# Two 1 MB tiles of the second layer asked for in five pieces of rows each

## The chip, the cores and the metric

The kernel runs on one core of a Trainium2 chip. The metric is the device time of one execution in microseconds (us), the median of several runs. The core has five engines that run their own instruction streams: PE (TensorE, matrix multiplication), DVE (VectorE), ACT (ScalarE), POOL (GpSimd) and SP (SyncE, which here does nothing but ask for transfers). Data come from the chip's main memory (HBM) into the on-chip memory by 16 DMA engines. A transfer is asked for by one instruction on SP and is finished when all its parts have landed; other engines learn of that from a semaphore.

## The reference

Two layers of a decoder that makes one token for each of 8 sequences: attention with 32 query heads over 4 groups of cached keys and values (4096 positions, 128 numbers each), and a dense layer with GELU. Both layers use the same weights and the same caches, all in 32-bit floats.

```python
def _A_ref(x, k_cache, v_cache, wq, wo):
    q = (x @ wq).reshape(B, Sq, Hq, Dh).transpose(0, 2, 1, 3)
    k = jnp.repeat(k_cache, rep, axis=1)
    v = jnp.repeat(v_cache, rep, axis=1)
    scores = jnp.einsum("bhqd,bhkd->bhqk", q, k) * (Dh ** -0.5)
    p = _softmax(scores, axis=-1)
    o = jnp.einsum("bhqk,bhkd->bhqd", p, v)
    return o.transpose(0, 2, 1, 3).reshape(B, Sq, Hq * Dh) @ wo

def _B_ref(x, w1, b1, w2, b2):
    h = _gelu(jnp.einsum("bsd,df->bsf", x, w1) + b1)
    return jnp.einsum("bsf,fd->bsd", h, w2) + b2

x = x + _A_ref(_layernorm(x), ...)   # layer 0
x = x + _B_ref(_layernorm(x), ...)
x = x + _A_ref(_layernorm(x), ...)   # layer 1
x = x + _B_ref(_layernorm(x), ...)
```

## The kernel before

Everything that is read passes through the arena, one tile of 128 partitions by 52 units; a unit is 1024 floats per partition (`SCW`, line 34), 512 KB over all partitions. A slot of the arena is 2, 4 or 8 units, so a transfer is 1, 2 or 4 MB; one of 2 units has rows of 8192 bytes, one row for each partition. The caches and weights lie in HBM in the order in which the tiles are read, so each row of a tile is one contiguous piece.

`stream` (line 255) is the list of all transfers in their order. It is filled before the first instruction (lines 770 to 796): wq, then for each sequence of layer 0 its K and V tiles, wo (`o0`), w1 (`i0`), w2, and then layer 1 with the sequences in reverse order, wo (`o1`), w1 (`i1`) and what is left of w2 (`late`). Each entry has a key, a size in units, its source and the units at which it may lie. `pump` (line 258) goes through the list in order: as long as the next entry's units are free, it takes the slot and issues one transfer on SP (line 268); the first entry without a place stops it. `release` (line 273) frees a slot after its last use and calls `pump` again. So the order of transfers is that of `stream`, and the moment of one is set by the buffer that it waits for.

All these transfers share SP's queue. The framework counts their completion on eight semaphores in turn (DMAHW0 to DMAHW7 in the order of instructions), so a transfer also waits until the one eight places before it, which used the same semaphore, has landed, where no other wait has shown that already.

The users of the two tiles that the change touches: `scores` (line 586) multiplies a K tile into the scores of one sequence, in layer 1 for sequence 6 with the tile ("k", 6, 3, 1) as the last of that sequence's eight pieces of K; it is 2 units at unit 36 (the list for `batch(1, last_b - 1, ...)`, line 786). `project` (line 418) multiplies the attention's output by wo; in layer 1 `o1` comes in six tiles of 8, 8, 8, 4, 2 and 2 units (line 791), numbered 0 to 5. After it comes `expand("i1")` (line 287), which multiplies by w1 (`i1`, tiles of five times 4, three times 2, and 1, 0.5 and 0.5 units, line 792; line 303 for the wide part, 306 for the rest) and, between these, by w2 (`down_row`, line 468, matmuls at line 472). Both end in one addition (line 846) and the transfer of the result (line 848).

Of the kernel before, what the change touches and what calls it, by code (L numbers as in the profile page):

```python
# [14 lines left out]
P = 128  # L15
# [34 lines left out]
Q_AT = (0, (B + 1) * QW - 32, (B + 1) * QW - 8, 32)  # L50
KEEP = SCW + CH + 3 * P
DMA_SCRATCH = 64


class Arena:
# [50 lines left out]
def decode_layers(ctx: ExitStack, tc: tile.TileContext, x, kc, vc, wq, wo, w1, w2, out):  # L106


    nc = tc.nc
# [148 lines left out]
    def pump():  # L258
        while stream:
            key, k, src, starts, keys = stream[0]  # L260
            if not k:
                slot = Kept(starts)
            else:
                slot = arena.take(k, [i for i in starts if i + k <= arena.limit])
            if slot is None:
                return
            stream.pop(0)
            nc.sync.dma_start(out=slot.ap[:, 0:src.shape[1]], in_=src)
            slot.cols = src.shape[1]
            slot.keys = keys  # L270
            held[key] = slot

    def release(slot):
        if slot.keys:
            held.update(slot.parts())
            return
        slot.free()
        pump()
# [424 lines left out]
    def opened():  # L703
        arena.limit = N_UNIT
        pump()
# [87 lines left out]
    for e, n in LATE:  # L793
        w = LATE_C * Q4
        at, to = CB * NFT * Q4 + e * w, LATE_AT * SCW + e * w
        stream.append((("late", e), 0 if e else LATE_C, w2[0][:, at:at + n * w], arena.ap[:, to:to + n * w] if e else (LATE_AT,), ()))
    pump()
    rs = layernorm(x_row, rsum)
    queries(rs)
# [123 lines left out]
```

## Time and profile before

| what | value |
|---|---|
| median of 3 runs | 848.6 us (847.54 to 849.02) |
| the profiled execution's own time | 848.87 us |
| its span, first to last instruction | 847.0 us |
| granted TensorE clock, mean | 0.821 of full speed |
| read from HBM in the span | 357.78 MB, 423 GB/s on average |
| transfers on SP's queue | 136 |
| TensorE, busy time on `scores` (L595) and `values` (L638) | 162.3 us and 87.4 + 84.9 us |

The span is shorter than the execution's own time, because what lies before the first and after the last instruction isn't in it. In the page's slices a digit is the busy share of one 21 us slice in tenths, and the DMA row is the mean over the 16 DMA engines. A queue's row has its packets, its megabytes and the time that its packets took as a share of 16 engines' span. In rows of instructions, what stands in brackets is the idle time of the engine just ahead and what ended it.

### The profile page before, as it was taken

How to read it: one execution, taken by the hardware profiler on the slowest of the kernel's cores; microseconds unless marked ns; L12 is line 12 of the kernel's file. 1: busy time of each engine (PE TensorE's matmuls, PEld its weight loads, DVE VectorE, ACT ScalarE, POOL GpSimd, SP SyncE). 2: the span in 40 equal slices, each digit the busy share in tenths (PEclk: the TensorE clock that was granted, in tenths of full speed). 3: DMA queues.
4: the chain of work that ended last, by engine and by line, in shares of the span. 5: the costliest groups of instructions: out<-in, count | busy, mean ns of one | idle time of the engine just before them, and what ended most of it. 6: DMA issues, size and time to landing. Idle time of an engine off the chain costs nothing.

```text
span 847.0 us, 9470 instructions
## 1 busy us (share of the span) xinstructions
PE 535.8 (63%) x4120; PEld 179.1 (21%) x4120; DVE 192.4 (23%) x636; ACT 55.4 (7%) x118; POOL 2.4 (0%) x14
## 2 busy tenths in 40 slices
PE   0755565656656657677778775476666576655677
PEld 0221111111111111133243222111111121212334
DVE  0013132313222231300010242232414132222011
ACT  0110000000000000000201100000000000000021
POOL 0000000000000000000000000000000000000000
PEclk9977779676876877699999897968768768788899
DMA  9999999999999999999999999999999999999997
GB/s 402 420 423 430 433 433 431 426 436 427 424 428 435 434 432 421 427 429 424 429 409 413 399 427 438 429 430 435 425 438 426 434 429 433 431 426 434 421 426 285
DMA packets 19768, 358.51 MB, mean 423 GB/s; under 512 B 2192, under 2 KB 2576, under 8 KB 4112
## 3 DMA queue, kind: packets, MB, share of 16 engines
q1 hardware_dynamic: 19584, 357.77, 99.2%
q8 instruction: 32, 0.52, 0.3%
q10 hardware_dynamic: 144, 0.15, 0.1%
q14 instruction: 8, 0.07, 0.0%
HBM read 357.78 MB, written 0.13 MB: 423 GB/s over the span
## 4 chain that ended last, share of the span: by engine, by line
DMA 73%; PE 23%; DVE 2%; issue 1%; another core or an unknown queue 1%; ACT 0%; SPq 0%; ACTq 0%; DVEq 0%
DMA arena<-in_k_dram 28%; DMA arena<-in_v_dram 21%; DMA arena<-in_w_dram 10%; DMA arena<-in_wo_dram 8%; PE sps L595 8%; PE o_ps L638 7%; DMA arena<-in_wq_dram 5%; PE y L424 2%; PE acc L361 1%; PE sps L472 1%; PE acc L306 1%; PE sps L650 1%; PE acc L303 0%; PE sps L346 0%
## 5 line engine op out<-in xcount | busy, mean ns | idle before, releaser
L595 PE MATMUL sps<-arena,qz 128*32 128x512 f32 x1024 | 162.3, 777 | 118.9 <-DMA arena<-in_k_dram 117.0
L638 PE MATMUL o_ps<-arena 128*32 128x512 f32 x512 | 87.4, 816 | 48.2 <-DMA arena<-in_v_dram 36.7
L638 PE MATMUL o_ps<-arena,spare 128*32 128x512 f32 x512 | 84.9, 782 | 40.9 <-DMA arena<-in_v_dram 34.0
L595 PEld LDWEIGHTS sps<-arena,qz 128*32 128x32 f32 x1024 | 37.7, 132 | 208.2 <-issue 169.8
L643 DVE SCALAR_TENSOR_TENSOR scr<-o_ps,bits,scr 128x128 f32<-128x128 f32 x192 | 67.3, 351 | 6.8
L641 DVE TENSOR_SCALAR scr<-o_ps,bits 128x128 f32<-128x128 f32 x64 | 22.4, 351 | 144.6 <-PE o_ps L638 144.6
L424 PE MATMUL y<-arena,oxT 128*32 128x256 f32 x512 | 37.8, 441 | 23.5 <-DMA arena<-in_wo_dram 23.5
L361 PE MATMUL acc<-arena,oxT 128*32 128x512 f32 x248 | 32.9, 671 | 6.3 <-DMA arena<-in_wq_dram 4.9
L650 PEld LDWEIGHTS sps<-bits,scr 128*128 128x128 f32 x128 | 21.7, 213 | 67.6 <-issue 48.3
L638 PEld LDWEIGHTS o_ps<-arena 128*32 128x32 f32 x512 | 16.9, 134 | 81.4 <-issue 49.1
L638 PEld LDWEIGHTS o_ps<-arena,spare 128*32 128x32 f32 x512 | 17.2, 131 | 71.7 <-issue 47.1
L600 DVE TENSOR_SCALAR_CACHE_REDUCE arena<-sps 128x512 f32<-128x512 f32 x16 | 11.1, 691 | 91.4 <-PE sps L595 91.4
L651 DVE TENSOR_TENSOR oxT<-sps,scr 128x8 f32<-128x8 f32 x64 | 10.5, 164 | 87.1 <-PE sps L650 87.1
L600 DVE TENSOR_SCALAR_CACHE_REDUCE spare<-sps 128x512 f32<-128x512 f32 x16 | 11.1, 691 | 82.4 <-PE sps L595 82.4
L619 ACT ACTIVATE sps<-arena,bits 128x512 f32<-128x512 f32 x16 | 10.9, 681 | 285.2 <-DVE scr L613 285.2
L619 ACT ACTIVATE sps<-spare,bits 128x512 f32<-128x512 f32 x16 | 10.9, 681 | 263.6 <-DVE scr L613 263.6
L650 PE MATMUL sps<-bits,scr 128*128 128x8 f32 x128 | 27.6, 288 | 0.0
L424 PEld LDWEIGHTS y<-arena,oxT 128*32 128x32 f32 x512 | 18.0, 125 | 44.0 <-DMA arena<-in_wo_dram 25.9
L303 PE MATMUL acc<-arena,oxT 128*32 128x512 f32 x160 | 20.7, 631 | 9.2 <-DMA arena<-in_w_dram 9.2
L184 PE MATMUL sps<-spare,ident 128*32 128x512 f32 (+2 forms) x60 | 24.9, 533 | 0.6 <-DVE scr L217 0.6
L609 PE MATMUL sps<-scr,bits 128*128 128x128 f32 x32 | 7.6, 322 | 22.9 <-DVE scr L605 22.9
L466 PE MATMUL sps<-arena,oxT 128*32 128x256 f32 x224 | 14.2, 382 | 5.6 <-DMA arena<-in_w_dram 5.6
(134 smaller groups left out, 248.8 us busy)
## 6 DMA issues: line engine op xcount, KB each, us to landing
arena<-in_v_dram SPq DMA_DIRECT2D x25, 4096.0 KB, 21.6
arena<-in_k_dram SPq DMA_DIRECT2D x21, 4096.0 KB, 20.6
arena<-in_k_dram SPq DMA_DIRECT2D x20, 2048.0 KB, 18.2
arena<-in_w_dram SPq DMA_DIRECT2D x16, 2048.0 KB, 12.7
arena<-in_v_dram SPq DMA_DIRECT2D x11, 2048.0 KB, 19.7
arena<-in_wo_dram SPq DMA_DIRECT2D x8, 2048.0 KB, 13.0
arena<-in_wo_dram SPq DMA_DIRECT2D x3, 4096.0 KB, 24.2
arena<-in_w_dram SPq DMA_DIRECT2D x6, 1024.0 KB, 19.6
```

The costliest lines, as they stand in the source:

```text
L184: nc.tensor.matmul(ps[0:32, 0:w], ident[:, 0:32], spare[:, 0:w], start=True, stop=True)
L303: nc.tensor.matmul(acc[32 * j:32 * j + 32, :], lhs, slot.ap[:, c:c + CH], start=(kt < 4), stop=(kt >= NT - 4))
L361: nc.tensor.matmul(acc[u][32 * j:32 * j + 32, d0 - j * CH:d1 - j * CH], xnT[:, kt * XS:kt * XS + 32], ap[:, d0 - c0:d1 - c0], start=(kt == ...
L424: nc.tensor.matmul(y[32 * j:32 * j + 32, 0:Q4], lhs[:, n * B:n * B + 32], slot.ap[:, c + j * Q4:c + (j + 1) * Q4], start=(n == 0), stop=(n ...
L466: nc.tensor.matmul(y[32 * g:32 * g + 32], h_at(kt), w2_at[c, kt], start=(n < 4), stop=(n >= NFT - 4))
L595: nc.tensor.matmul(ps[32 * g:32 * g + 32, :], qz[:, c:c + 32], kt[:, g * CH:(g + 1) * CH], start=(j == 0), stop=(j == HKV - 1))
L600: nc.vector.tensor_scalar(st["row", b].ap[:, half * CH:(half + 1) * CH], ps, SCALE, None, op0=ALU.mult, op1=ALU.max, accum_out=st["mx", b] ...
L619: nc.scalar.activation(pp, row[:, h * CH:(h + 1) * CH], AF.Exp, bias=bias, scale=1.0, accum_out=ls[:, h:h + 1])
L638: nc.tensor.matmul(o[32 * g:32 * g + 32, :], s[:, g], v[:, g * CH:(g + 1) * CH], start=(half == 0), stop=(half == NH - 1))
L641: nc.vector.tensor_scalar(r, o[:, 0:P], sel_t[:, 0:1], None, op0=ALU.mult)
L643: nc.vector.scalar_tensor_tensor(r, o[:, t * P:(t + 1) * P], sel_t[:, t:t + 1], r, op0=ALU.mult, op1=ALU.add)
L650: nc.tensor.matmul(po[:, 0:REP], r_s[j % 2], sel_h, start=True, stop=True)
```

## The change

`pump` looks up each entry's key in a new table, `CUT`. For two keys the tile is asked for in five transfers that take the tile's rows from the top, piece by piece; every other tile is asked for in one transfer of 128 rows, as before. The slot, the source, the order of `stream` and the arithmetic stay as they are.

```diff
@@ -50,6 +50,7 @@
 KEEP = SCW + CH + 3 * P
 DMA_SCRATCH = 64
+CUT = {(1, ("k", 6, 3, 1)): (96, 10, 10, 7, 5), (("o1",), 4): (96, 10, 10, 8, 4)}
@@ -265,7 +266,10 @@
             if slot is None:
                 return
             stream.pop(0)
-            nc.sync.dma_start(out=slot.ap[:, 0:src.shape[1]], in_=src)
+            r0 = 0
+            for n in CUT.get(key, (P,)):
+                nc.sync.dma_start(out=slot.ap[r0:r0 + n, 0:src.shape[1]], in_=src[r0:r0 + n])
+                r0 += n
             slot.cols = src.shape[1]
             slot.keys = keys
             held[key] = slot
```

On SP, where the K tile is asked for: `arena<-in_k_dram 128x2048` is the tile ("k", 6, 3, 1), 2048 floats in each of 128 rows; a name in `waits` is what the transfer waits for, DMAHW a completed transfer, PE a buffer that TensorE has read. Before:

```order
L268 DMA arena<-in_k_dram 128x4096 [waits DMAHW3_49,PE_49]
L268 DMA arena<-in_k_dram 128x2048 [waits PE_49]
L268 DMA arena<-in_v_dram 128x8192
L268 DMA arena<-in_v_dram 128x8192 [waits DMAHW7_49,DMAHW5_49,PE_49]
L268 DMA arena<-in_k_dram 128x4096 [waits DMAHW0_49,PE_49]
```

After the change, at the same place:

```order
L271 DMA arena<-in_k_dram 128x4096 [waits DMAHW3_49,PE_49]
L271 DMA arena<-in_k_dram 96x2048 [waits PE_49]
L271 DMA arena<-in_k_dram 10x2048 x2
L271 DMA arena<-in_k_dram 7x2048
L271 DMA arena<-in_k_dram 5x2048 [waits DMAHW4_49]
L271 DMA arena<-in_v_dram 128x8192 [waits DMAHW5_49]
L271 DMA arena<-in_v_dram 128x8192 [waits DMAHW7_49,DMAHW6_49,PE_49]
L271 DMA arena<-in_k_dram 128x4096 [waits DMAHW2_49,DMAHW3_49,DMAHW1_49,DMAHW4_49,DMAHW0_49,PE_49]
```

One transfer has become five, the two V tiles of 4 MB stand four places further back, and the later K tile that takes the same units waits for five completions instead of one.

On SP, at the end of wo in layer 1 and the beginning of w1 (`in_w_dram`): the first `128x2048` of the pair is tile 4 of `o1`, the second tile 5, and the `128x4096` behind them are tiles 0 to 4 of `i1`. Before:

```order
L268 DMA arena<-in_wo_dram 128x8192 [waits DMAHW3_49,PE_49]
L268 DMA arena<-in_wo_dram 128x4096 [waits DMAHW4_49,PE_49]
L268 DMA arena<-in_wo_dram 128x2048 [waits PE_49] x2
L268 DMA arena<-in_w_dram 128x4096 [waits DMAHW5_49,PE_49]
L268 DMA arena<-in_w_dram 128x4096 [waits PE_49]
L268 DMA arena<-in_w_dram 128x4096 [waits DMAHW6_49,PE_49]
L268 DMA arena<-in_w_dram 128x4096 [waits PE_49]
L268 DMA arena<-in_w_dram 128x4096 [waits DMAHW7_49,PE_49]
L268 DMA arena<-in_w_dram 128x2048 [waits DMAHW0_49,PE_49]
```

After the change:

```order
L271 DMA arena<-in_wo_dram 128x8192 [waits DMAHW7_49,PE_49]
L271 DMA arena<-in_wo_dram 128x4096 [waits DMAHW0_49,PE_49]
L271 DMA arena<-in_wo_dram 96x2048 [waits PE_49]
L271 DMA arena<-in_wo_dram 10x2048 x2
L271 DMA arena<-in_wo_dram 8x2048
L271 DMA arena<-in_wo_dram 4x2048
L271 DMA arena<-in_wo_dram 128x2048 [waits DMAHW1_49,PE_49]
L271 DMA arena<-in_w_dram 128x4096 [waits DMAHW2_49,PE_49]
L271 DMA arena<-in_w_dram 128x4096 [waits DMAHW3_49,PE_49]
L271 DMA arena<-in_w_dram 128x4096 [waits DMAHW4_49,PE_49]
L271 DMA arena<-in_w_dram 128x4096 [waits DMAHW5_49,PE_49]
```

Tile 4 is five transfers. The tiles behind it wait for transfers that stand closer to them: tile 5 of `o1` for `o1` tile 1, tile 0 of `i1` for `o1` tile 2 (semaphore DMAHW2), tile 1 of `i1` for `o1` tile 3 (DMAHW3), and tile 2 of `i1` for the 96 rows (DMAHW4).

On PE, in `project` of layer 1, at the matmuls that read tiles 4 and 5 of `o1`. Before:

```order
L424 MATMUL y<-arena,oxT 32x256 [waits DMAHW7_49]
L424 MATMUL y<-arena,oxT 32x256 x15
L424 MATMUL y<-arena,oxT 32x256 [waits DMAHW0_49]
L424 MATMUL y<-arena,oxT 32x256 x7
L424 MATMUL y<-arena,oxT 32x256 [waits DMAHW1_49]
L424 MATMUL y<-arena,oxT 32x256 x7
```

After the change (line 428 is line 424 of before):

```order
L428 MATMUL y<-arena,oxT 32x256 [waits DMAHW3_49]
L428 MATMUL y<-arena,oxT 32x256 x15
L428 MATMUL y<-arena,oxT 32x256 [waits DMAHW6_49,DMAHW5_49,DMAHW7_49,DMAHW4_49,DMAHW0_49]
L428 MATMUL y<-arena,oxT 32x256 x7
L428 MATMUL y<-arena,oxT 32x256 [waits DMAHW1_49]
L428 MATMUL y<-arena,oxT 32x256 x7
```

The first matmul on tile 4 waits for five completions instead of one; the order of TensorE's instructions is the same. The matmuls on the K tile wait in the same way. The streams of DVE, ACT and POOL are the same as before.

## Prediction

> **What bounds the kernel now.** I read the page first: the busy shares, the 40 slices and the queues.
>
> ```profile
> span 847.0 us, 9470 instructions
> ...
> PE 535.8 (63%) x4120; PEld 179.1 (21%) x4120; DVE 192.4 (23%) x636; ACT 55.4 (7%) x118; POOL 2.4 (0%) x14
> ...
> DMA  9999999999999999999999999999999999999997
> GB/s 402 420 423 430 433 433 431 426 436 427 424 428 435 434 432 421 427 429 424 429 409 413 399 427 438 429 430 435 425 438 426 434 429 433 431 426 434 421 426 285
> ...
> q1 hardware_dynamic: 19584, 357.77, 99.2%
> q8 instruction: 32, 0.52, 0.3%
> ...
> DMA 73%; PE 23%; DVE 2%; issue 1%; another core or an unknown queue 1%; ACT 0%; SPq 0%; ACTq 0%; DVEq 0%
> ```
>
> The transfers fill the span: SP's queue q1 holds 99.2% of 16 DMA engines' time, TensorE is busy 63%, and the chain of waits is 73% DMA. So only two things can change the time: how many bytes an engine carries, and how late the last engine is. The bytes are the same after the change. From the q1 row: 357.77 MB in 0.992 x 16 x 847.0 us = 13,444 engine-us is 26.6 GB/s for one engine, so **one row of 8192 bytes costs an engine 0.308 us**. The 136 transfers of SP with 128 rows each make 136 x 128 = 17,408 packets, and 19,584 - 17,408 = 2,176 = 136 x 16 more: 16 completions per transfer. So a transfer of 128 rows is 16 engines with 8 rows each.
>
> Next, how the stream ends: the windows view, with the DMA share (mean over the 16 engines) last but one in a row, after TensorE's granted clock.
>
> ```profile
> 512.00:780.00 268.00, 164.41 (x1011) 50.22 (x1015) 74.89 (x241) 10.63 (x28) 0.00 (x0) 0.77 1.00 431
> 780.00:812.00 32.00, 18.10 (x236) 8.57 (x232) 1.51 (x6) 1.79 (x3) 0.00 (x0) 0.86 1.00 422
> 812.00:836.00 24.00, 20.75 (x282) 9.89 (x278) 3.03 (x13) 6.22 (x13) 0.00 (x0) 0.98 1.00 420
> ...
> 838.00:839.00 1.00, 1.00 (x40) 0.92 (x36) 0.00 (x0) 0.00 (x0) 0.00 (x0) 1.00 0.91 344
> 839.00:840.00 1.00, 1.00 (x40) 0.83 (x32) 0.00 (x0) 0.00 (x0) 0.00 (x0) 1.00 0.68 264
> 840.00:841.00 1.00, 1.00 (x36) 0.83 (x32) 0.00 (x0) 0.00 (x0) 0.00 (x0) 1.00 0.55 203
> 841.00:842.00 1.00, 1.00 (x28) 0.51 (x24) 0.32 (x1) 0.23 (x1) 0.00 (x0) 1.00 0.29 111
> 842.00:843.00 1.00, 1.00 (x25) 0.60 (x23) 0.00 (x0) 0.00 (x0) 0.00 (x0) 1.00 0.03 12
> ```
>
> From 512 to 836 no engine has a gap (share 1.00). Then they stop one after the other between 838 and 842.5, although each has had the same rows of every tile. The mean engine ends at 838 + 0.91 + 0.68 + 0.55 + 0.29 + 0.03 = 840.46, the last near 842.5: **the engines stand some 4 us apart, and the last one is 2.0 us behind the mean**. What puts them apart stands in the queues view of 780 to 847 us:
>
> ```profile
> q1 hardware_dynamic: 2786, 25.36, 90.2%
> q8 instruction: 5, 0.08, 0.5%
> ```
>
> Five instruction packets of 16 KB took 0.005 x 16 x 67 = 5.4 engine-us, 1.07 us each (1.27 by the 0.3% of the whole span). A packet falls on one engine and is not shared, and 32 of them on 16 engines need not fall evenly. One packet is about 4 rows of 8 KB (4 x 0.308 = 1.23 us).
>
> Last, whether the late engines set the end: the chain of waits from 800 us, then TensorE in order of time (in brackets: idle time before it and what ended that).
>
> ```profile
> 802.66 27.81 DMA arena<-in_w_dram
> 830.47 0.04 issue
> 830.52 1.92 PE acc L303 x16
> ...
> 841.20 2.68 PE sps L472 x48
> 843.87 0.02 issue
> 843.90 0.42 DVE xb L846
> ```
>
> ```profile
> 824.97 1.93 PE L303 MATMUL acc<-arena,oxT 128*32 128x512 f32 x16 [0.27 <-DMA arena<-in_w_dram]
> 826.71 1.91 PE L472 MATMUL sps<-arena,oxT 128*32 128x256 f32 x32
> 828.55 0.66 PE L398 MATMUL sps<-ident,scr 128*128 128x128 f32 x4
> 830.52 1.92 PE L303 MATMUL acc<-arena,oxT 128*32 128x512 f32 x16 [1.31 <-DMA arena<-in_w_dram]
> ```
>
> The fifth 2 MB tile of w1 (i1 tile 4) lands at 830.5 and TensorE has waited 1.31 us for it. From there to 843.87 TensorE is the chain, 13.35 us with almost no wait. So the end hangs on the slowest engine at i1 tile 4, and with the data there TensorE could have started at 829.21 at the earliest.
>
> **The change part by part.** *Rows per engine.* A piece of 10 rows is 10 packets and reaches at most 10 engines; 96 rows are 6 on each of 16. If every piece begins at the same first engine, with one row per engine, the K tile gives 10 rows to engines 0-4, 9 to 5-6, 8 to 7-9 and 6 to 10-15; the wo tile 10 to 0-3, 9 to 4-7, 8 to 8-9 and 6 to 10-15. Against 8 + 8, engines 0-3 carry 4 rows more, 4 carries 3, 5-6 two, 7 one, 8-9 none, and 10-15 carry 4 fewer: -1.23 us on six engines, +1.23 us at most on five. No row of this trace shows a piece under 128 rows, so between "no shift at all" (pieces dealt round) and this I take this one, since a queue that starts each of its transfers anew is the plain reading. [...]
>
> *What it is worth.* If the six relieved engines are the late ones, i1 tile 4 lands 1.23 us sooner, TensorE's wait falls from 1.31 to 0.08 us, and the 13.35 us behind it move up whole; the last tile, for which TensorE waits 0.20 us at 843.12, comes off the same engines and moves with it:
>
> ```profile
> 843.12 0.23 PEld L472 LDWEIGHTS sps<-arena,oxT 128*32 128x32 f32 x8 [0.20 <-DMA arena<-in_w_dram]
> ```
>
> More than 1.31 + 0.27 = 1.58 us isn't there for the taking at these two waits, whatever the transfers do. The profile gives no engine's number, so that the late ones are 10-15 is an assumption; the rivals price the others.
>
> *What it adds.* Eight more issues on SP, at both places in front of other transfers.
>
> ```profile
> 501.55 0.33 SPq L268 DMA_DIRECT2D arena<-in_k_dram  x1
> 501.93 10.10 SPq L268 DMA_DIRECT2D arena<-in_v_dram  x2
> ...
> 789.43 43.86 SPq L268 DMA_DIRECT2D arena<-in_w_dram  x14
> ```
>
> ```profile
> 512.18 1.06 PE L595 MATMUL sps<-arena,qz 128*32 128x512 f32 x8 [0.54 <-DMA arena<-in_k_dram]
> ...
> 795.53 7.07 PE L424 MATMUL y<-arena,oxT 128*32 128x256 f32 x96 [4.45 <-DMA arena<-in_wo_dram]
> 802.92 1.07 PE L424 MATMUL y<-arena,oxT 128*32 128x256 f32 x16 [0.32 <-DMA arena<-in_wo_dram]
> 805.40 1.07 PE L424 MATMUL y<-arena,oxT 128*32 128x256 f32 x16 [1.41 <-DMA arena<-in_wo_dram]
> ...
> 810.38 1.94 PE L303 MATMUL acc<-arena,oxT 128*32 128x512 f32 x8 [2.62 <-DMA arena<-in_w_dram]
> ```
>
> One issue follows another in 0.38 us, so the V tile behind the K tile is asked for 1.5 us later. The K tile itself, issued at 501.55, is used at 512.18: some 10 us of transfers stand ahead of the V tile, and 1.5 us hides there. Behind the wo tile the eight completion counters come round sooner, as the order of SP shows: i1 tile 0 now waits for wo tile 2 (landed by 795.5) instead of being asked for at 789.43, i1 tile 1 for wo tile 3 (landed by 802.9). What covers that is the queue: when wo tile 2 has landed, wo tiles 3 to 5 (4 MB, 9.9 us at the row price) still stand ahead of i1 tile 0, less the 4 us by which the first engine leads, so 5.9 us for one issue. The same sum for i1 tile 1 gives wo tiles 4 and 5 and i1 tile 0, again 9.9 - 4. If the cover were gone, every engine would idle for what is missing, one for one; I cost it at nothing. TensorE must collect five completions at each tile: it waits 0.54 and 1.41 us for data there anyway, and 2.62 us again at 810.38. The added completions are a few packets on engines 0-4. I put 0 to 0.1 us for all of it and take 0.03.
>
> *Sum.* 848.87 us is the profiled execution's own time, its span 847.00 and 1.87 around it. 847.00 - 1.23 + 0.03 = 845.80, so 847.67 by that execution; it lies 0.27 above the median of 848.6, and against the median the forecast is **847.4 us**.
>
> **The rivals.** *A. The pieces collide where they are written: slower.* The 0.308 us may belong not to the engine but to the place in the on-chip memory that a row goes to; 128-row transfers cannot tell, as each engine then has its own 8 rows. [...] For it: the rate never passes 438 GB/s in any slice, as if a common limit held. Against it: nothing in this trace. [...]
>
> *B. The late engines are the low-numbered ones.* Then the rows are put on top: +1.23 us where four are added, +0.6 where the last engine takes two; the middle gives **849.5 us**. Nothing in the rows speaks for or against it.
>
> *C. It doesn't shift what matters.* The pieces are dealt round, or the last engine at 830.5 is among 8-9, or instruction packets after 830 fall elsewhere: the 1.31 us wait stays, 0 +- 0.4 us, **848.6 us**.
>
> **How the numbers follow.** Forecast 45%, own range 846.8 to 848.2 (gain 1.6 to 0.6, and 0.2 of noise below); A 25%; B 10%; C 20%. 0.2% is 1.7 us, about what a measurement of this kernel can tell from no change: 846.9 and 850.3 are the marks. The forecast lies inside them and only its lower edge reaches 846.9: faster 0.08. Slower is A without its low end: 0.22. The rest, 0.70, is within. For 8 in 10 the range must hold forecast, B, C and about half of A: 846.8 to 851.8.
>
> **What would show it.** In the profile after, the wait before TensorE's L303 at 830 falls towards 0.1 us, and the DMA share between 838 and 843 falls from 1 to 0 within some 2.5 us instead of 4: right. A steeper fall with a later end, or a DMA share of 1.00 with fewer GB/s in the slices at 510 and 800: A. A longer tail: B. The same tail: C. A share below 1.00 between 780 and 812 would show the cover of the issues gone. The forecast is wrong if the q1 share rises for the same bytes, since then a row has become dearer.

## The result, and the profile after

| | before | after |
|---|---|---|
| median of 5 runs beside each other | 848.61 us (847.54 to 849.65) | 858.72 us (857.19 to 859.74) |
| span of the profiled execution | 847.0 us | 856.8 us |

The ratio is 1.0117, 95% interval 1.0102 to 1.0132: **10.1 us slower**. The forecast was 847.4, its range ended at 851.8.

First the page after the change: span, gigabytes per second in 40 slices, and SP's queue.

```profile
span 856.8 us, 9487 instructions
...
DMA  9999999999999999999999999999999999999997
GB/s 398 418 431 427 436 417 437 421 437 431 421 433 428 437 431 425 420 429 427 427 403 421 425 356 415 439 428 431 431 429 433 432 429 428 436 429 431 300 427 285
...
q1 hardware_dynamic: 19648, 357.77, 99.2%
```

The queue moves the same 357.77 MB at the same share, 99.2%, of a span that is 9.8 us longer: the engines are as full as before, and the same bytes keep them busy longer. Two slices stand out, 356 (before: 427) around 500 us and 300 (before: 421) around 800 us, the places of the two tiles. The queue has 19,648 - 19,584 = 64 packets more. If a transfer of n rows uses 16, 10, 10, 7, 5 and 16, 10, 10, 8, 4 engines, each tile has 48 completions instead of 16, which is 64 more in all. So the count fits, as a sum, the number of engines per piece that was forecast.

Next the two places in windows (engines' busy times, granted TensorE clock, DMA share, GB/s), after the change:

```profile
506.00:510.00 4.00, 2.82 (x25) 0.69 (x25) 0.87 (x3) 0.00 (x0) 0.00 (x0) 1.00 1.09 242
510.00:514.00 4.00, 2.68 (x16) 0.59 (x16) 0.00 (x0) 0.00 (x0) 0.00 (x0) 0.63 1.12 234
514.00:518.00 4.00, 1.85 (x16) 0.19 (x8) 0.57 (x1) 0.00 (x0) 0.00 (x0) 0.93 0.95 389
518.00:780.00 262.00, 157.65 (x967) 48.44 (x971) 74.22 (x240) 10.63 (x28) 0.00 (x0) 0.79 1.00 431
...
800.00:804.00 4.00, 4.00 (x40) 1.81 (x40) 0.00 (x0) 0.00 (x0) 0.00 (x0) 0.50 1.05 219
804.00:808.00 4.00, 1.82 (x28) 0.72 (x20) 0.00 (x0) 0.00 (x0) 0.00 (x0) 0.92 0.97 213
808.00:812.00 4.00, 3.04 (x32) 1.39 (x32) 0.00 (x0) 0.00 (x0) 0.00 (x0) 0.50 1.02 238
```

and the same windows of before:

```profile
506.00:510.00 4.00, 1.83 (x20) 0.42 (x16) 0.70 (x2) 0.00 (x0) 0.00 (x0) 1.00 1.09 457
510.00:514.00 4.00, 2.71 (x24) 0.42 (x16) 0.69 (x2) 0.00 (x0) 0.00 (x0) 1.00 1.02 440
514.00:518.00 4.00, 0.46 (x2) 0.30 (x2) 2.29 (x9) 1.52 (x4) 0.00 (x0) 0.76 0.95 410
800.00:804.00 4.00, 3.67 (x66) 1.72 (x56) 0.00 (x0) 0.00 (x0) 0.00 (x0) 1.00 1.05 442
804.00:808.00 4.00, 1.80 (x28) 1.05 (x28) 0.77 (x5) 0.00 (x0) 0.00 (x0) 1.00 1.01 422
808.00:812.00 4.00, 1.62 (x8) 0.45 (x12) 0.74 (x3) 1.79 (x3) 0.00 (x0) 0.70 1.00 426
```

The DMA share is about 1 in both (a packet counts whole in the window where it begins, so single windows pass 1), but the rate halves, and between the two places it is 431 GB/s as ever. The bytes that are missing at the K tile are 4 us x ((457 - 242) + (440 - 234) + (410 - 389)) GB/s = 1.77 MB, or 4.1 us at 431 GB/s; at the wo tile 4 x (223 + 209 + 188) = 2.48 MB, or 5.8 us. Together that is 9.9 us: the whole loss lies in these two stretches of 12 us.

The chain of waits at the end:

```profile
783.43 29.74 DMA arena<-in_wo_dram
...
813.24 27.08 DMA arena<-in_w_dram
...
840.36 1.93 PE acc L307 x16
...
853.74 0.42 DVE xb L850
```

`i1` tile 4 starts at 840.36 instead of 830.52, and the last addition at 853.74 instead of 843.90: both 9.84 us later. What lies between is unchanged (13.38 us). So the stream is late by the whole amount when the last tiles come, and the end only passes it on. The windows of the tail, and TensorE's row at `i1` tile 4 in order of time:

```profile
847.00:848.00 1.00, 1.00 (x24) 0.60 (x20) 0.16 (x1) 0.23 (x1) 0.00 (x0) 1.00 0.97 379
848.00:849.00 1.00, 1.00 (x40) 0.97 (x36) 0.00 (x0) 0.00 (x0) 0.00 (x0) 1.00 0.86 332
849.00:850.00 1.00, 1.00 (x39) 0.83 (x34) 0.00 (x0) 0.00 (x0) 0.00 (x0) 1.00 0.68 260
850.00:851.00 1.00, 1.00 (x36) 0.81 (x30) 0.00 (x0) 0.00 (x0) 0.00 (x0) 1.00 0.46 168
851.00:852.00 1.00, 1.00 (x26) 0.45 (x18) 0.32 (x1) 0.23 (x1) 0.00 (x0) 1.00 0.24 90
852.00:853.00 1.00, 1.00 (x24) 0.58 (x20) 0.00 (x0) 0.00 (x0) 0.00 (x0) 1.00 0.03 10
```

```profile
840.36 1.93 PE L307 MATMUL acc<-arena,oxT 128*32 128x512 f32 x16 [0.68 <-DMA arena<-in_w_dram]
```

The mean engine ends at 847 + 0.97 + 0.86 + 0.68 + 0.46 + 0.24 + 0.03 = 850.24, the last at 852.4 by the trace's packet records: 2.2 us apart, about as before. The fall takes some 5 us, not the 2.5 us that the forecast asked for. TensorE's wait did shrink, from 1.31 to 0.68 us, but that says nothing by itself when the whole stream has moved by 9.84.

### The profile page after: what moved, and what is told of

It is laid out like the page before. It is cut to its first block, busy times and chain, and to the rows that moved or that the text cites. A ratio compares the mean times of both kernels' runs of the same rounds, so it can differ in the third digit from the quotient of the medians.

```text
span 856.8 us, 9487 instructions
## 1 busy us (share of the span) xinstructions
PE 540.2 (63%) x4120; PEld 179.5 (21%) x4120; DVE 192.6 (22%) x636; ACT 55.6 (6%) x118; POOL 2.4 (0%) x14
## 3 DMA queue, kind: packets, MB, share of 16 engines
q1 hardware_dynamic: 19648, 357.77, 99.2%
## 4 chain that ended last, share of the span: by engine, by line
DMA 74%; PE 22%; DVE 1%; issue 1%; another core or an unknown queue 1%; SPq 0%; ACT 0%; ACTq 0%; DVEq 0%
DMA arena<-in_k_dram 26%; DMA arena<-in_v_dram 22%; DMA arena<-in_wo_dram 12%; DMA arena<-in_w_dram 10%; PE sps L599 8%; PE o_ps L642 7%; DMA arena<-in_wq_dram 5%; PE y L428 1%; PE acc L365 1%; PE sps L476 1%; PE acc L310 1%; PE sps L654 1%; PE acc L307 0%; SPq L271 0%
## 5 line engine op out<-in xcount | busy, mean ns | idle before, releaser
L599 PE MATMUL sps<-arena,qz 128*32 128x512 f32 x1024 | 167.2, 798 | 125.5 <-DMA arena<-in_k_dram 124.4
L642 PE MATMUL o_ps<-arena 128*32 128x512 f32 x512 | 84.3, 790 | 45.9 <-DMA arena<-in_v_dram 34.4
L428 PE MATMUL y<-arena,oxT 128*32 128x256 f32 x512 | 41.3, 468 | 26.9 <-DMA arena<-in_wo_dram 26.9
L655 DVE TENSOR_TENSOR oxT<-sps,scr 128x8 f32<-128x8 f32 x64 | 10.6, 165 | 93.1 <-PE sps L654 93.1
L623 ACT ACTIVATE sps<-arena,bits 128x512 f32<-128x512 f32 x16 | 10.9, 681 | 283.5 <-DVE scr L617 283.5
L623 ACT ACTIVATE sps<-spare,bits 128x512 f32<-128x512 f32 x16 | 10.9, 681 | 272.0 <-DVE scr L617 272.0
```

Source lines behind the costliest of these rows:

```text
L428: nc.tensor.matmul(y[32 * j:32 * j + 32, 0:Q4], lhs[:, n * B:n * B + 32], slot.ap[:, c + j * Q4:c + (j + 1) * Q4], start=(n == 0), stop=(n ...
L599: nc.tensor.matmul(ps[32 * g:32 * g + 32, :], qz[:, c:c + 32], kt[:, g * CH:(g + 1) * CH], start=(j == 0), stop=(j == HKV - 1))
L623: nc.scalar.activation(pp, row[:, h * CH:(h + 1) * CH], AF.Exp, bias=bias, scale=1.0, accum_out=ls[:, h:h + 1])
L642: nc.tensor.matmul(o[32 * g:32 * g + 32, :], s[:, g], v[:, g * CH:(g + 1) * CH], start=(half == 0), stop=(half == NH - 1))
```

## The experiments

Four readings were set against each other. **The forecast's theory**: a row costs its engine 0.308 us wherever it is written. **P**, the rival A of the prediction: the cost belongs to the place in the on-chip memory, and rows that share a place get in each other's way. **N**: each transfer, or each small one, has a price of its own. **S**: SP's issues and the eight completion counters hold the stream up. Two more come in on the way: **Q**, any transfer of under 128 rows is slow, and **R**, the reading from HBM is what is slow. In the diffs `K` is the key `(1, ("k", 6, 3, 1))` and `O` is `(("o1",), 4)`; what isn't shown is as in the changed kernel.

**Each tile alone.**

```diff
-CUT = {K: (96, 10, 10, 7, 5), O: (96, 10, 10, 8, 4)}
+CUT = {K: (96, 10, 10, 7, 5)}        # e1
+CUT = {O: (96, 10, 10, 8, 4)}        # e2
```

> Only the K tile is cut (96, 10, 10, 7, 5). [...] Theory N (each added transfer costs a fixed time, 10.1 us / 8 = 1.26 us): 4 x 1.26 = +5 us. Theory S (SP asks too late): gaps in the DMA share, size open. This run splits the loss; it does not decide between P and N.

> Only the wo tile is cut (96, 10, 10, 8, 4). P: the stretch at 800 to 812 us moved 223 GB/s instead of 431, 12 x (1 - 223/431) = 5.8 us: +6 us, and together with the run on the K tile the 10.1 us of the change. N: 4 x 1.26 = +5 us. If the row shift itself (4 rows fewer on late engines) is worth something, the two parts together come out above or below the whole by about 1 us.

Measured: 853.54 us, 1.0067 (1.0049 to 1.0085), and 853.86 us, 1.0066 (1.0051 to 1.0082), beside 849.03 before. Each tile costs some 5 us and the two add up. The K tile is used some 330 us before the end, so its loss is one of the stream, not of the tail.

**Five transfers, whole columns.** As many transfers, issues and semaphores as in the change, but all of 128 rows:

```diff
-                nc.sync.dma_start(out=slot.ap[r0:r0 + n, 0:src.shape[1]], in_=src[r0:r0 + n])
+                nc.sync.dma_start(out=slot.ap[:, r0:r0 + n], in_=src[:, r0:r0 + n])   # n: 512, 512, 512, 256, 256
```

> Both tiles in five transfers each, but cut by columns (512, 512, 512, 256, 256 floats of all 128 rows): the same eight added transfers, the same issues and semaphores on SP, every engine with its own rows. P: 0 +- 0.5 us. N: +10 us. S: +10 us.

Measured: 848.93 us, 1.0004 (0.9995 to 1.0014). Its windows at the two places:

```profile
510.00:515.00 5.00, 3.37 (x22) 0.88 (x14) 1.34 (x5) 0.00 (x0) 0.00 (x0) 1.00 1.03 440
...
800.00:805.00 5.00, 3.39 (x60) 1.69 (x48) 0.00 (x0) 0.00 (x0) 0.00 (x0) 1.00 1.05 428
```

The rate stays whole. Eight more transfers, their completions and the counters that come round sooner cost nothing that can be measured: S falls, and so does N in the form of a price for each transfer.

**Halves, and 96 + 32.** Only two transfers for each tile, both of neighbouring rows:

```diff
+CUT = {K: (64, 64), O: (64, 64)}     # e4
+CUT = {K: (96, 32), O: (96, 32)}     # e9
```

> Both tiles in two transfers of 64 rows: every engine gets 4 + 4 rows, so no load is moved, two transfers are added. [...] N: 2 x 1.26 = +2.5 us. S: 0.

> Both tiles as 96 neighbouring rows and 32 neighbouring rows, none of the small pieces. If the 96 neighbouring rows carry the loss: 1.008 to 1.012 (+7 to +10 us). If the small pieces of 10, 10, 7 and 5 rows carry it: 1.003 or less (+2.5 us).

Measured: 859.65 us, 1.0136 (1.0114 to 1.0159), for the halves, beside 849.03; 859.14 us, 1.0114 (1.0099 to 1.0130), for 96 + 32, beside 848.58. Windows of the halves, then of 96 + 32:

```profile
510.00:515.00 5.00, 3.13 (x16) 0.51 (x16) 0.00 (x0) 0.00 (x0) 0.00 (x0) 0.74 1.05 239
...
800.00:805.00 5.00, 4.60 (x44) 2.17 (x48) 0.00 (x0) 0.00 (x0) 0.00 (x0) 0.50 1.01 236
```

```profile
510.00:515.00 5.00, 3.51 (x16) 0.59 (x16) 0.00 (x0) 0.00 (x0) 0.00 (x0) 0.66 1.07 261
...
800.00:805.00 5.00, 5.00 (x60) 2.28 (x56) 0.00 (x0) 0.00 (x0) 0.00 (x0) 0.54 1.02 220
```

Without any small piece, and with 16 completions for each transfer as in those of 128 rows (e9's queue has 19,616 packets, 32 more than before), the loss is all there. So the pieces of 10 and fewer rows aren't needed for it. Pieces of 96, 64 or 32 neighbouring rows are enough. What the halves cost is taken up below.

**The same halves, rows apart.** Transfers of 64 and of 32 rows that are spread over the whole memory:

```diff
+                for i in range(2):      # e10; e13 has 4 transfers, i:P:4
+                    nc.sync.dma_start(out=slot.ap[i:P:2, 0:src.shape[1]], in_=src[i:P:2])
```

> Both tiles in two transfers of 64 rows, but of every second row (0, 2, 4, ... and 1, 3, 5, ...) instead of the upper and the lower half, in HBM and on the chip. Number of transfers, rows per transfer and rows per engine are those of the run with halves (+10.6 us); only which rows go together differs. [...] Theory Q (any transfer of under 128 rows runs slowly, whatever its rows): +10.6 us. Theory R (the reading from HBM): not +10.6, size open.

> [...] Q: at least the +10.6 us of two transfers, since more pieces are under 128 rows. R: open.

Measured: 849.26 us, 1.0011 (0.9999 to 1.0024), and 848.69 us, 1.0002 (0.9993 to 1.0012), beside 848.78. Windows of every second row:

```profile
510.00:515.00 5.00, 2.29 (x18) 0.48 (x10) 1.63 (x7) 0.00 (x0) 0.00 (x0) 0.98 1.02 441
...
800.00:805.00 5.00, 3.27 (x60) 1.57 (x54) 0.00 (x0) 0.00 (x0) 0.00 (x0) 1.00 1.04 439
```

64 rows cost 10.6 us as neighbours and nothing that can be told from noise when every second row is taken. A transfer of fewer than 128 rows is no loss in itself, so Q falls. P named the right side: which rows go together decides.

**Read or written?** Rows apart in HBM are also apart in the on-chip memory; these two take one without the other, so the rows of the two tiles stand permuted:

```diff
+                    nc.sync.dma_start(out=slot.ap[i * 64:i * 64 + 64, 0:src.shape[1]], in_=src[i:P:2])   # e11
+                    nc.sync.dma_start(out=slot.ap[i:P:2, 0:src.shape[1]], in_=src[i * 64:i * 64 + 64])   # e12
```

> Both tiles written as two halves of 64 neighbouring rows, but read from every second row of HBM; the rows of both tiles thereby stand in another order. P: as the halves, +10.6 us. R: as every second row on both sides. Q: +10.6 us.

> Both tiles written into every second row, read from 64 neighbouring rows of HBM; their rows stand in another order. [...] R: as the halves, +10.6 us. Q: +10.6 us.

Measured: 858.54 us, 1.0112 (1.0097 to 1.0127), for neighbours written and every second row read; 848.73 us, 0.9995 (0.9986 to 1.0004), for the reverse. The order in which HBM is read doesn't matter; which rows are written together does.

**Eight pieces of 16 rows, the K tile alone.** The same two questions with smaller pieces, which answer neither:

```diff
+                for i in range(8):      # near = i * 16:i * 16 + 16, apart = i:P:8
+                    # e5: write near, read near     e6: write apart, read apart
+                    # e7: write near, read apart    e8: write apart, read near
```

> Only the K tile, in eight transfers of 16 neighbouring rows (0-15, 16-31, ...): every engine has one row of each, so no load is moved. [...] N: 7 x 1.26 = +8.8 us. [...]

> As the run with 16 neighbouring rows, but each of the eight transfers takes every eighth row (j, j + 8, ...), in HBM and on the chip. [...] N: +8.8 us, the same as with neighbouring rows. R: faster or slower than neighbouring rows as the reading goes.

> Eight transfers into 16 neighbouring rows each, but from every eighth row of HBM; the rows of this K tile thereby stand in another order, so its scores are those of permuted rows. [...] N: +8.8 us.

> The other way round: eight transfers into every eighth row, from 16 neighbouring rows of HBM; the rows of this K tile stand in another order here too. [...] N: +8.8 us.

Measured, beside 849.11: 852.83 (1.0036, 1.0024 to 1.0048), 854.00 (1.0050, 1.0032 to 1.0067), 852.24 (1.0037, 1.0025 to 1.0049) and 852.91 us (1.0042, 1.0027 to 1.0057). All four lose 3 to 5 us, less than N's 8.8. The window of e6:

```profile
510.00:515.00 5.00, 2.10 (x16) 0.40 (x12) 0.67 (x2) 0.00 (x0) 0.00 (x0) 0.80 0.73 134
```

A DMA share of 0.73 is idle time; outside this group the lowest share in this window is 0.90 (e14). Eight small transfers take all eight completion counters, so the next tile waits until the first of them has landed; that is the likely cause of the idle time and wasn't tried by itself. But idle time is the smaller part. In the packet records rows took longer too, which makes 2.5, 3.6, 2.7 and 2.7 us of the four losses (the sum is explained with the table below). So pieces of 16 rows are slow in both forms, and every eighth row is a bad spread of its own, unlike every second and every fourth. That neighbours are no slower here than rows apart is against P and stays open. The large pieces of e10 to e13 decide the two questions; these don't.

**Do moved rows pay when rows lie apart?** The forecast's own term, -1.23 us, can't be seen beside the loss. These kernels write most of a tile as every second row (64) and every fourth (32), and the last 32 rows so that, by the forecast's assumption, rows move from engines 10 to 15 to the others as in the change (e14, e16), or don't move (e15, e17):

```diff
+            for a in CUT.get(key, (slice(0, P),)):
+                nc.sync.dma_start(out=slot.ap[a, 0:src.shape[1]], in_=src[a])
+    # CUT of both tiles begins with slice(0, P, 2), slice(1, P, 4); behind them
+    # e14, K:  slice(3, 43, 4), slice(43, 83, 4), slice(83, 111, 4), slice(111, P, 4)   10, 10, 7, 5 rows
+    # e14, wo: slice(3, 43, 4), slice(43, 83, 4), slice(83, 115, 4), slice(115, P, 4)   10, 10, 8, 4 rows
+    # e15:     slice(3, 67, 4), slice(67, P, 4)                                         16, 16 rows
+    # e16:     slice(3, 112, 12), slice(7, 116, 12), slice(11, 120, 12), slice(123, P, 4)   10, 10, 10, 2 rows
+    # e17:     slice(3, P, 4)                                                           32 rows
```

> Both tiles in five or six transfers whose rows lie apart: every second row (64), then every fourth (32), then the other 32, every fourth, in pieces of 10, 10, 7, 5 (K) and 10, 10, 8, 4 (wo). The small pieces move rows between the engines as the change does, but no transfer writes neighbouring rows. Forecast's theory, that a row costs its engine the same wherever it is written: the moved rows now pay, 0.9986 (-1.23 us), and below the control e15 by as much. Place theory with a place that is as fast as its engine: each place keeps its bytes whoever brings them, so 1.000, the same as e15. If the small pieces lose by themselves, above 1.003.

> The control of e14: the same first two transfers of each tile, the last 32 rows in two pieces of 16, every engine one row of each, so no row is moved between engines. Both theories: 1.000 (within 0.001); above 1.003 if small transfers lose by themselves.

> Both tiles as 64 rows (every second), 32 rows (every fourth), then the other 32 as 10, 10, 10 (every twelfth row, spread over the whole memory) and 2 rows. As in the change engines 10 to 15 have 4 rows fewer in all, engines 0 to 9 two or four more; no piece is crowded. Forecast's theory: below the control e17 by 1.23 us, ratio to it 0.9986. Place theory with places as fast as engines: same as e17 within 0.0007. Above e17 by over 1 us: small pieces lose however they lie, or the late engines are not 10 to 15.

> The control of e16: both tiles as 64 rows (every second) and twice 32 rows (every fourth), all engines with 4, 2 and 2 rows of each tile. 1.000 within 0.001 by both theories.

Measured: 851.88 (1.0032, 1.0022 to 1.0042) against its control's 850.83 us (1.0018, 1.0010 to 1.0027); 852.14 (1.0037, 1.0024 to 1.0051) against its control's 848.88 us (1.0002, 0.9993 to 1.0011). No gain shows in either pair: the medians are 1.05 and 3.26 us above the control, where the forecast's theory has 1.23 below. But all except e17 missed the place theory's 1.000 too, the control e15 by 2.25 us. Each of e15's two small pieces lies in one half of the tile (rows 3 to 63 and 67 to 127), as e4's halves do, so it is no clean control; only e16 and e17 spread their pieces of 10 and more rows over the memory. And e16 has four small pieces where e17 has one of 32 rows, so the pair differs in the size of the pieces and not only in the moved rows. Windows of e16, then of its control:

```profile
510.00:515.00 5.00, 2.19 (x20) 0.32 (x12) 0.78 (x3) 0.00 (x0) 0.00 (x0) 1.00 1.00 372
...
800.00:805.00 5.00, 3.37 (x56) 1.46 (x48) 0.00 (x0) 0.00 (x0) 0.00 (x0) 0.98 1.00 274
```

```profile
510.00:515.00 5.00, 2.99 (x24) 0.60 (x24) 0.62 (x2) 0.00 (x0) 0.00 (x0) 1.00 1.09 467
...
800.00:805.00 5.00, 5.00 (x84) 2.53 (x76) 0.00 (x0) 0.00 (x0) 0.00 (x0) 0.88 1.02 426
```

The small pieces slow the stream at full DMA share even with their rows 12 apart. The packet records of the trace say the same. They give each packet's start, time and size; here are the rows of 8192 bytes between 799 and 811 us:

```
kernel                    mean us   longest us
before                    0.31      0.32
e13, every fourth         0.31      0.32
e17, control              0.31      0.32
e15, pieces of 16         0.35      0.54
e16, pieces of 10 apart   0.44      0.72
e9, 96 + 32               0.57      0.98
after                     0.59      0.98
```

The same records account for nearly the whole loss. Take what rows of 8, 16 and 32 KB took beyond 0.313, 0.616 and 1.217 us (about their means before the change), add it up around the two tiles (490 to 530 and 780 to 820 us) and share it among 16 engines. That is 10.5 us in the changed kernel, 10.9 in e4, 9.2 in e9 and in e11, 3.3 in e16, 3.0 in e14, 1.8 in e15 and nothing (within 0.1) in e10, e12, e13 and e17; the medians lost 10.1, 10.6, 10.6, 9.8, 3.5, 3.3, 2.3 and at most 0.5 us. The cut tiles have rows of 8 KB only, but 4.9 of e4's 10.9 us lie in rows of 16 and 32 KB: tiles in flight beside a cut one are slowed too.

**A long stretch.** To tell a lower rate from a price for each cut, 16 MB in a row, the four 4 MB tiles of sequence 4 in layer 1, in halves of neighbouring rows, and nothing else cut:

```diff
+            cut = key[0] == 1 and key[1][:2] in (("k", 4), ("v", 4))
+            for r0, n in ((0, 64), (64, 64)) if cut else ((0, P),):
```

> The four 4 MB tiles of sequence 4 in layer 1 (16 MB in a row) in two transfers of 64 neighbouring rows each, everything else as before. [...] If each MB in halves costs what it did in e4 (5.3 us): +85 us, 933 us. If engines that are out of step hide it: under +10 us.

Measured: 892.67 us, 1.0517 (1.0498 to 1.0537), 44.0 us above 848.68. The page's slices and a window in the middle:

```profile
GB/s 394 435 425 423 430 428 432 429 437 428 425 434 422 438 421 430 425 429 426 404 403 429 433 425 433 329 210 210 210 368 425 433 435 424 433 436 426 423 427 277
```

```profile
600.00:640.00 40.00, 12.72 (x72) 3.53 (x68) 6.39 (x19) 1.52 (x4) 0.00 (x0) 0.66 1.00 210
...
660.00:700.00 40.00, 24.51 (x150) 7.29 (x142) 11.89 (x39) 1.52 (x4) 0.00 (x0) 0.83 1.00 430
```

A flat 210 GB/s at a DMA share of 1.00: this is a second limit, half of 431, and not a price for a cut. 16.8 MB take 79.9 us at 210 and 38.9 at 431, 41.0 more; the remaining 3.0 us fit the stretch's edges, where tiles that aren't cut are in flight beside cut ones: between 540 and 670 us 553 rows of 32 KB took over 1.4 us, and the cut tiles have only 512. The same sum fits the halves of one tile (e4): 1.05 MB at half rate is 2.5 us more, and with some 3 us of edges 5.5 us a tile, 11 for both, against 10.6 measured.

## Why the prediction was wrong

It got the sign wrong; of its cases, rival A (25%) has the sign, and the side, which is the written one (e11 and e12: 9.8 us against nothing).

*What bounds the kernel*: right. The DMA share stays 1.00, and 9.9 us of missing bytes became 9.8 us of span. But "only two things can change the time: how many bytes an engine carries, and how late the last engine is" is **where it failed**. A third thing can, the time that an engine needs for a row. "One row of 8192 bytes costs an engine 0.308 us" was measured on transfers of 128 rows alone, and was carried over to transfers of another shape as if it belonged to the engine. In the changed kernel the mean is 0.59 us between 799 and 811 us, and e18 shows the lower rate by itself.

*Rows per engine*: the counts of engines per piece fit the 64 added completions. That each piece begins at the same engine, so that the same six carry 4 rows fewer, was the author's assumption and is not shown, nor that the late engines are 10 to 15, nor that instruction packets are what puts the engines apart.

*What it is worth*, -1.23 us: no run shows it. e14 and e16 lie above their controls, by 1.05 and 3.26 us, but they have smaller pieces than these too, so whether moved rows by themselves would pay stays open. If a place is as slow as an engine, they can't pay: a row that another engine brings is still written to the same place, whose load stays the same, and now two engines share it. That reading is argued from e16's longer packets at the control's number of rows; no run here names the place a packet went to.

*What it adds*, 0 to 0.1 us: right. The DMA share at 780 to 812 us has no gap, and e3 with as many issues and completions measures 1.0004.

*Rival A*: its side stands for large pieces (e10 to e13, e18): what decides is which rows are written together. That they share a place is inferred from the half rate, 210 GB/s against 431. The size of A that the range takes in by half is shown by no run; the runs showed 10.1 us for the change, and 10.6 us with 96 + 32 alone (e9). Nor do engines that are out of step absorb it: the distance between the mean and the last engine stays some 2 us (2.0 before, 2.2 after), and transfers beside the cut tile are slowed as well, some 3 us for each stretch by e4 and e18. Its sign, a DMA share of 1.00 with fewer GB/s at 510 and 800, is what came.

*The chances*: 0.22 for slower rested on "against it: nothing in this trace". No row of it showed a transfer of neighbouring rows under 128, so the trace spoke neither for nor against A, and the range's upper end should have taken in all of A and not half.

*Left open*: why the edges of a stretch cost as much as some 3 us, and why e16's pieces lose although their rows lie 12 apart. A guess of the author's, which no run shows, is that in a transfer of 128 rows, and in every second or fourth row, each engine writes to a place of its own, while a small piece, or a half of neighbouring rows, sends it to a place that another engine is writing to. It fits e3, e10, e13 (no loss) and e4, e9, e14 to e16 (loss), but the profile gives neither the engine nor the place of a packet. No kernel here beat the one before: the best, e12, measures 0.9995 with an interval over 1.

## What to carry to other kernels

A price per row or per byte that a saturated queue shows holds for the shape of transfer that it was measured on: here a row of 8 KB took 0.31 us before and 0.59 us around the cut wo tile. A tile that has to be cut is better cut by columns, or into every second or fourth partition, which cost nothing here (1.0004, 1.0011 and 1.0002 in e3, e10 and e13), than into neighbouring partitions (1.0136 in e4). Look at GB/s beside the DMA share: here engines that were all busy at half the rate (210 GB/s at a share of 1.00, e18) were held up on the written side (e11, e12). And where a limit may belong to the destination, don't count on a gain from moving work between the engines that serve it: none showed here (e14 and e16, whose smaller pieces leave the question open).

## What the runs showed of the hardware that was not expected

- 64 neighbouring rows to a transfer hold the whole stream at 210 GB/s, for as long as such transfers follow one another (e18), while 64 rows of every second partition run at 439 to 441 (e10, windows of 5 us around the cut tiles).
- The loss is of the written side alone: reading every second row of HBM and writing neighbours costs 9.8 us, the reverse nothing (e11, e12).
- One cut tile of 1 MB costs twice what the half rate explains (5.3 us against 2.5, e4), and 4.9 of the 10.9 us by which rows took longer there lie in tiles that weren't cut; over 16 MB this extra is 3 us in 44 (e18).
- Rows that lie apart aren't enough: pieces of 10 rows, 12 apart, cost 3.3 us beside their control (e16), and 16 rows, every eighth, run at 134 GB/s in 5 us with a DMA share of 0.73 (e6).
